# Turning the tail's exponentials with the fourth tile's, by sixteen moves inside SBUF, in an attention and feed-forward kernel

## The chip, the cores and the metric

The kernel runs on one core of one Trainium2 chip. The time is in device microseconds (us), the median of several executions. Next to it stands one profiled execution, with its own time and its span, which is the time from the first to the last instruction. Each query of the trace shows that execution.

The engines are named as in the profile: PE is TensorE (matrix products), PEld its weight loads, DVE is VectorE, ACT is ScalarE, POOL is GpSimd, and SP is SyncE, which here issues nearly all transfers (DMAs).

## The reference

```python
def _attn_ref(q, k, v, f):                    # q, k, v: 8 x 8 x 576 x 64; f: 8 x 8 x 576
    scores = scale * np.matmul(q, k.transpose(0, 1, 3, 2))
    cum = np.cumsum(np.log(np.clip(f, 0.0001, 1.0)), axis=-1)
    decay = cum[:, :, :, None] - cum[:, :, None, :]
    scores = np.where(causal, -1e9, scores + decay)
    attn = np.exp(scores - np.max(scores, axis=-1, keepdims=True))
    attn = attn / (np.sum(attn, axis=-1, keepdims=True) + 1e-09)
    return np.matmul(attn, v)

def _moe_ref(x, w_in, w_out, alpha):          # x: 4608 x 512; w_in: 512 x 2048; w_out: 2048 x 512
    h = x @ w_in
    g = np.maximum(h, 0.0) + alpha * np.minimum(h, 0.0)
    return g @ w_out
```

Eight batches of eight heads of causal attention with a decay feed a two-layer network. All values are float32.

## The kernel before

Attention is worked off in 32 pairs of heads (4 pairs in each of 8 batches), `attention(n)` for n from 0 to 31. The queries of a head are cut into four tiles of 128 and a tail of 64. The two tails of a pair are put together into one block of 128 rows, so that a pair has nine row blocks: four tiles for each head and one common tail. For a block the steps are these:

- TensorE makes the scores (for n of 4 and more from a split of Q and K into two parts each, three products).
- VectorE adds the decay (`Z` and `Zt`, spread to all rows by loads from DRAM) and finds the extreme of each row.
- ScalarE makes the exponentials and their row sums (`expo`, line 508).
- The exponentials are transposed, so that keys stand on the partitions, and go to the value product.

The transposing is done in two ways. The first is TensorE's: `blocks` (line 521) multiplies by the identity into a PSUM bank, and `evac` (lines 516 and 517) copies the bank to SBUF. Tiles 0, 1 and 2 and the tail (`tail`, lines 548 to 551) go this way. The second serves the fourth tile (i = 3) of a pair that is `turned`, which before the change are pairs 8 to 31: SP stores the exponentials of both heads to a DRAM buffer `ex` (line 659), loads them back in four loads (line 660) that put blocks of 32 rows side by side in `em`, and VectorE's stream transpose turns 32 x 32 blocks into `eT3_` (line 665). Keys then stand in another order on the partitions, and V is loaded a second time in that order (`vs`, line 497). In pairs 0 to 7 the fourth tile goes through TensorE too.

The value product of a pair (`prods_of`, line 687) is not run on its own: from pair 3 on it is put behind the scores of tile 2 of the next pair, in one step of TensorE (`stretch`, line 617).

When the four pairs of a batch are done, the first feed-forward product for that batch (`ffn1`, line 783) can run: 16 output blocks of 12 products of 512 columns. Its result goes through ScalarE and VectorE (lines 800 to 805) into a DRAM buffer (line 807). The second product (`ffn2`) comes after all attention. The weights `w_in` are converted at the start, by ScalarE, VectorE and GpSimd (`split64`, lines 306 to 329).

The order of the instructions on every engine is fixed when the kernel is built. `Plan.run` (line 115) places the steps one after the other: of the steps that are ready first it takes the one of the smallest key. It reckons a duration for each step, 400 ns or so for an issue on SP, and for transfers one common channel with a rate (line 160). A `Ring` hands out the buffers. On the chip the engines keep the order and wait for each other with semaphores.

Names that the text below uses: `eT` are transposed exponentials, `vr` is V, `rq` and `rk` are the loads of Q and K, `rd` and `ri` carry the reciprocals of the row sums, `hd` the results of the first product, `xx` and `wi` are the operands of the first feed-forward product, `turn` is the step with the stream transpose.

Of the kernel before, what the change touches and what calls it, by code (L numbers as in the profile page):

```python
# [29 lines left out]
NX = (8, B * NP)  # L30
# [53 lines left out]
class Plan:  # L84
# [30 lines left out]
    def run(self):  # L115
# [7 lines left out]
        while left:  # L123
# [63 lines left out]
def attention_moe(  # L187
    ctx: ExitStack,
    tc: tile.TileContext,
    qq: bass.AP,  # L190
    kk: bass.AP,
    vv: bass.AP,
    vs: bass.AP,
# [20 lines left out]
    ex = [dram.tile([2, 128, 512], F32, name=f"ex{i}") for i in range(2)]  # L214
# [32 lines left out]
    rrq = ring(sp, 2, [128, QW], F32, "rq")  # L247
    rrk = ring(sp, 2, [128, S], F32, "rk")
    rZ = Ring(Store([(sp.tile([128, 2, ZW], F32, name=f"Z{i}"), sp.tile([128, S], F32, name=f"Zt{i}")) for i in range(2)]))
    rvr = ring(sp, 2, [128, 5, 2, D], F32, "vr")  # L250
    rT1 = ring(sp, 3, [128, 384], F32, "eT1_")
    rT2 = ring(sp, 4, [128, 4, 192], F32, "eT2_")
# [5 lines left out]
    re3 = ring(sp, 1, [128, 2, 512], F32, "e3_")  # L258
# [5 lines left out]
    rwr = ring(sp, 2, [128, 512], U64, "wr")  # L264
    rwa = ring(sp, 1, [128, 512], U32, "wa")
# [7 lines left out]
    wbf = sp.tile([128, 512], BF16, name="wbf")  # L273
    sel = sp.tile([9, 6, 128], F32, name="sel")
# [150 lines left out]
    def load_n(n, held):  # L425
# [4 lines left out]
        bq, bk, bZ = Buf(rrq), Buf(rrk), Buf(rZ)  # L430
        kq = -99 if first else -59 if n == 1 else kl
        dq = [] if first else [o_scan]
        l_q = op("SP", 450, lambda: sy.dma_start(bq.t, qq[b, p]), kq, dq, [bq], kb=320)
        l_k = op("SP", 450, lambda: sy.dma_start(bk.t, kk[b, p]), kq, dq, [bk], kb=288)
        Z, Zt = (lambda: bZ.t[0]), (lambda: bZ.t[1])
        rz = []
        for h in range(2):
            if first:
# [12 lines left out]
        if first:  # L451
# [13 lines left out]
        if n < NN:  # L465
            held += [bq, bk]
            return [l_q, l_k], rz, rt, bZ, [(lambda: bq.t, lambda: bk.t)]
# [3 lines left out]
        for hi, lo, raw, ld, w in ((Qh, Ql, bq, l_q, QW), (Kh, Kl, bk, l_k, S)):  # L471
            o1 = op("ACT", c_acs(w), lambda hi=hi, raw=raw: ac.activation(hi(), raw.t, AF.Copy), kc, [ld], [raw, bQ])  # L472
            o2 = op("POOL", c_po(w), lambda hi=hi, lo=lo, raw=raw: po.tensor_tensor(lo(), raw.t, hi().bitcast(F32), ALU.subtract), kc, [o1], [raw, bQ])  # L473
            out += [o1, o2]
# [3 lines left out]
    waiting, behind, later_x = [], [], []  # L478

    def attention(n):  # L480
# [9 lines left out]
        bv = Buf(rvr)  # L490
        l_v = op("SP", 400, lambda: sy.dma_start(bv.t, vv[b, p]), kl + 1, [o_scan], [bv], kb=320)
        nt_ = 3 if n >= NN else 4
        bT1, bT2 = [Buf(rT1) for _ in range(2)], [Buf(rT2) for _ in range(2)]
        b3, bT3, turned = Buf(re3), Buf(rT3), NX[0] <= n < NX[1]
        if turned:
            bm, bvs = Buf(rm3), Buf(rvs)
            l_s = op("SP", 400, lambda: sy.dma_start(bvs.t, vs[b, p]), kl + 12, [o_scan], [bvs], kb=256)
# [27 lines left out]

        def tail(st):

            bt = Buf(re)
            prev = None
            for g in range(2):  # L530
# [9 lines left out]
                def red(bS=bS, ks=ks, g=g):  # L540
                    ve.tensor_tensor_reduce(out=bt.t[:, ks], in0=bS.t[:, :288], in1=bZ.t[1][:, ks],  # L541
                                            scale=-0.125, scalar=lo()[:, 9:10] if g else 3.0e38, op0=ALU.add, op1=ALU.min,
                                            accum_out=lo()[:, 4:5] if g else lo()[:, 9:10])
# [16 lines left out]
        def quick(bR, r_, key):  # L560
# [11 lines left out]
            q_ = op("PE", 1400, prods, key, [r_, o_sel], bB + [bR])  # L572
            for c0, c1 in ((0, 512), (512, S)):
# [30 lines left out]
        def stretch(tiles, st):  # L604
# [16 lines left out]
            s_0.append(s)  # L621
            done(s)
# [4 lines left out]
        def tile(h, i, st, bS, s, c0):  # L627
# [4 lines left out]
            at = (lambda t: t[:, h]) if i == 3 else (lambda t: t)  # L632
# [21 lines left out]
            if i == 3 and turned:  # L654
                if h == 0:
                    return
                d = ex[n % 2]
                key = k0 + 7.8
                o_ = op("SP", 400, lambda: sy.dma_start(d.rearrange("h q k -> q h k"), b3.t), key, [be[0][3][1], nm], [b3], kb=512)
                got = [op("SP", 400, lambda k=k: sy.dma_start(  # L660
                    bm.t[32 * k : 32 * k + 32], d[:, :, 128 * k : 128 * k + 128].rearrange("h (a c) s -> c (h a) s", c=32)),
                    key + 0.1, [o_], [bm], kb=128) for k in range(4)]
                for h_ in range(2):
                    def turn(h_=h_):
                        ve.transpose(bT3.t[:, h_].rearrange("p s (a c) -> p a s c", a=4),
                                     bm.t[:, 4 * h_ : 4 * h_ + 4].rearrange("p a (s r) -> p a s r", r=32))

                    e3.append(op("DVE", c_tr(512), turn, k0 + 13.5, got, [bm, bT3]))
                return
            if i >= 2:  # L670
# [3 lines left out]
                def tr2():  # L674
                    blocks(bT.t, 0, at(b1.t), range(i + 1))
                    if last:
                        pe.transpose(bT.t[0:64, 384:512], bt.t[:, 512:S], ident)  # L677

                t = op("PE", (i + 1 + last) * 109, tr2, st + 0.3, [nm, o_id] + ([nt] if last else []), [bT, b1] + ([bt] if last else []))
                to, tb = ((lambda: bT3.t[:, h]), bT3) if i == 3 else ((lambda: bT2[h].t[:, 0 : i + 1, 0:128]), bT2[h])  # L680
# [6 lines left out]
        def prods_of(r, out):  # L687

            def pv():
                both = []  # L690
                o = out()
                for h in range(2):
                    e1_, e2_ = bT1[h].t, bT2[h].t
                    if r == 0:
                        both.append([(0, 0, 256, e1_[:, 0:256]), (1, 128, 256, e1_[:, 256:384])])
                    else:
                        both.append([(j, 0, 128, e2_[:, j, 0:128]) for j in range(3)]
# [118 lines left out]
    for fc in range(NF):  # L816
        load_w_in(fc)
# [294 lines left out]
```

## Time and profile before

| | us |
|---|---|
| median of 3 runs | 1072.73 |
| lowest and highest run | 1070.98, 1072.88 |
| profiled execution, its time | 1073.41 |
| profiled execution, its span | 1071.6 |
| TensorE busy | 1054.9 |
| VectorE busy | 738.6 |
| ScalarE busy | 675.0 |
| GpSimd busy | 280.5 |

Busy time is the time in which an engine has at least one instruction running. Matrix products are pipelined: their recorded durations overlap, so the distance from the start of one to the start of the next is a better price than the duration. A row of the grouped view gives line, engine, operation, what is written and read, the shape and the count, and then the busy time, the mean duration, and the idle time just before with what ended it. The mean granted clock of TensorE is 0.992.

### The profile page before, as it was taken

What the parts mean: (1) busy time and instruction counts of PE and PEld (TensorE: products, weight loads), DVE (VectorE), ACT (ScalarE), POOL (GpSimd) and SP (SyncE); (2) the same over time, 40 slices, a digit from 0 to 9 for tenths busy, and PEclk for the clock granted to TensorE, in tenths of its full rate; (3) what the DMA queues carried; (4) which work ended last, traced back from release to release, by engine and by line L of the source; (5) the groups of instructions that cost most, each with busy time, mean ns of one, the idle gap of its engine ahead of it and who ended that gap; (6) DMA issues with size and microseconds to landing.
All of it is one profiled execution on the core that took longest, in us unless ns stands there. A gap on an engine that the chain in (4) does not pass through costs nothing.

```text
span 1071.6 us, 22543 instructions
## 1 busy us (share of the span) xinstructions
PE 1054.9 (98%) x8132; PEld 916.7 (86%) x8132; DVE 738.6 (69%) x1680; ACT 675.0 (63%) x1590; POOL 280.5 (26%) x407
## 2 busy tenths in 40 slices
PE   8889989999999999999999999999999999999998
PEld 5678867888888888888788888899999999999998
DVE  6788864555544545545544599779988898989994
ACT  6879877786766766667655375656454554646551
POOL 6578574553433434344221000000000000000000
PEclk9989999999999999999999999999999999999999
DMA  6967778987887986886763666464444443444411
GB/s 181 268 194 235 225 217 232 271 264 238 253 237 214 259 241 203 242 247 212 215 198 129 204 214 225 167 199 139 136 126 132 137 137 120 138 130 126 140 60 40
DMA packets 152441, 202.15 MB, mean 189 GB/s; under 512 B 18930, under 2 KB 89481, under 8 KB 152329
## 3 DMA queue, kind: packets, MB, share of 16 engines
q1 hardware_dynamic: 152041, 200.51, 61.3%
q8 instruction: 64, 1.05, 0.4%
q14 instruction: 48, 0.39, 0.1%
q10 hardware_dynamic: 288, 0.20, 0.1%
HBM read 139.55 MB, written 61.11 MB: 187 GB/s over the span
## 4 chain that ended last, share of the span: by engine, by line
PE 92%; DMA 2%; POOL 2%; DVE 1%; issue 1%; ACT 1%; SPq 0%; DVEq 0%; POOLq 0%
PE bank L332 86%; PE bank L521 5%; DMA Z<-c 2%; PE bank L392 1%; POOL Z L447 1%; DMA wr<-in_w_in_dram 0%; POOL wi L328 0%; POOL Z L448 0%; PE bank L677 0%; DVE eT L516 0%; DVE wa L322 0%; POOL Z L449 0%; ACT e L508 0%; POOL Ql L473 0%; POOL Kl L473 0%
## 5 line engine op out<-in xcount | busy, mean ns | idle before, releaser
L332 PE MATMUL bank<-xx,wi 128*128 128x512 f32 x1728 | 428.4, 397 | 2.3 <-ACT wi L327 1.8
L332 PEld LDWEIGHTS bank<-xx,wi 128*128 128x128 f32 x1728 | 314.4, 188 | 68.7 <-issue 4.8
L805 DVE SCALAR_TENSOR_TENSOR hs<-bank,sa,hs 128x512 f32<-128x512 f32 x96 | 71.2, 743 | 109.9 <-ACT hs L803 109.8
L332 PE MATMUL bank<-wot,xx 128*128 128x256 f32 x1008 | 123.9, 283 | 0.0
L332 PE MATMUL bank<-wi,xx 128*128 128x256 f32 x1008 | 123.9, 283 | 0.0
L332 PEld LDWEIGHTS bank<-wot,xx 128*128 128x128 f32 x1008 | 122.3, 192 | 0.0
L332 PEld LDWEIGHTS bank<-wi,xx 128*128 128x128 f32 x1008 | 122.3, 192 | 0.0
L508 ACT ACTIVATE e<-e,st 128x512 f32<-128x512 f32 (+2 forms) x160 | 109.2, 685 | 4.2 <-DVE st L541 2.0
L803 ACT ACTIVATE hs<-bank,ab 128x512 f32<-128x512 f32 x96 | 66.0, 688 | 63.4 <-PE bank L332 62.6
L517 ACT ACTIVATE eT<-bank 128x384 f32<-128x384 f32 (+2 forms) x192 | 83.3, 461 | 34.7 <-PE bank L332 20.1
L725 POOL TENSOR_TENSOR xx<-xs,xx 128x256 fp32r<-128x256 f32 x64 | 49.0, 783 | 136.6 <-ACT xx L723 136.4
L473 POOL TENSOR_TENSOR Ql<-rq,Qh 128x640 fp32r<-128x640 f32 x28 | 45.1, 1611 | 137.8 <-ACT Qh L472 89.7
L332 PE MATMUL bank<-eT,vr 128*64 128x128 f32 (+2 forms) x1408 | 80.0, 263 | 0.2 <-DVE eT L516 0.2
L332 PEld LDWEIGHTS bank<-eT,vr 128*64 128x64 f32 x1408 | 63.9, 138 | 14.1 <-issue 7.1
L447 POOL TENSOR_TENSOR Z<-Z,tri 128x384 f32<-128x384 f32 x64 | 60.0, 945 | 45.5 <-DMA Z<-c 31.2
L999 ACT ACTIVATE xx<-gx 128x1024 fp32r<-128x1024 f32 x48 | 50.8, 1058 | 30.8 <-PE bank L332 15.1
L521 PEld LDWEIGHTS bank<-ident,e 128*128 128x128 f32 x384 | 46.9, 146 | 20.5 <-issue 5.3
L521 PE MATMUL bank<-ident,e 128*128 128x128 f32 x384 | 62.2, 287 | 1.9 <-DVE st L639 1.6
L1002 DVE TENSOR_TENSOR xx<-gx,xx 128x1024 fp32r<-128x1024 f32 x48 | 58.6, 1220 | 7.4 <-ACT xx L999 7.4
L332 PE MATMUL bank<-wi,gh 128*128 128x256 f32 x504 | 62.4, 283 | 0.0
L332 PE MATMUL bank<-wot,gh 128*128 128x256 f32 x504 | 62.4, 283 | 0.0
L332 PEld LDWEIGHTS bank<-wot,gh 128*128 128x128 f32 x504 | 61.4, 192 | 0.1
(140 smaller groups left out, 1777.6 us busy)
## 6 DMA issues: line engine op xcount, KB each, us to landing
hd<-hs SPq DMA_DIRECT2D x144, 256.0 KB
wx<-hd SPq DMA_DIRECT2D x47, 512.0 KB
Z<-c SPq DMA_DIRECT2D x62, 256.0 KB
hr<-hd SPq DMA_DIRECT2D x25, 512.0 KB
ex<-e SPq DMA_DIRECT2D x24, 512.0 KB
em<-ex SPq DMA_DIRECT2D x96, 128.0 KB
rq<-in_qq_dram SPq DMA_DIRECT2D x32, 320.0 KB
vr<-in_vv_dram SPq DMA_DIRECT2D x32, 320.0 KB
```

Of the source, the lines that this page charges most:

```text
L332: pe.matmul(o, lhsT, rhs, start=start, stop=stop)
L392: op("PE", 800, lambda: [pe.matmul(bw.t, wbf[:, 0:128], wbf, start=True, stop=True) for _ in range(3)], -200, [o_wbf], [bw])
L447: m1 = op("POOL", c_po(128 * 3), lambda z4=z4: po.tensor_tensor(z4()[:, 6:9], z4()[:, 0:3], tb(3), ALU.add), kc + 0.1, got + [o_mask], [bZ])
L473: o2 = op("POOL", c_po(w), lambda hi=hi, lo=lo, raw=raw: po.tensor_tensor(lo(), raw.t, hi().bitcast(F32), ALU.subtract), kc, [o1], [raw, bQ])
L508: ex = op("ACT", c_exp(w), lambda: ac.activation(at(bt.t)[:, :w], at(bt.t)[:, :w], AF.Exp, bias=lo()[:, col : col + 1], scale=-1.0, accum_ ...
L517: return op("ACT", c_act(w), lambda: ac.activation(dst(), src(), AF.Copy), key, deps, [bank] + bufs)
L521: pe.transpose(t[:, c : c + 128], src[:, 128 * j : 128 * j + 128], ident)
L725: xl = op("POOL", c_po(256), lambda r=r, t0=t0: po.tensor_tensor(bx.t[:, 1, t0 : t0 + 256], bxs[r].t[:, 0:256], bx.t[:, 0, t0 : t0 + 256]. ...
L803: cp = op("ACT", c_act(512), lambda bh=bh, bs=bs, fc=fc: ac.activation(bs.t, bh.t, AF.Relu, scale=ab[:, fc : fc + 1]), -1000, [last, o_sg] ...
L805: cp = op("DVE", c_dve(512), lambda bh=bh, bs=bs, fc=fc: ve.scalar_tensor_tensor(bs.t, bh.t, sa[:, fc : fc + 1], bs.t, ALU.mult, ALU.add), ...
L999: his.append(op("ACT", c_acs(128 * GW * (j1 - j0)), lambda j0=j0, j1=j1, src=src, o_=o_: ac.activation(o_(0, j0, j1), src(), AF.Copy), key ...
L1002: rdy.append(op("DVE", c_dve(128 * GW * (j1 - j0)), lambda j0=j0, j1=j1, src=src, o_=o_: ve.tensor_tensor(o_(1, j0, j1), src(), o_(0, j0, ...
```

## The change

- Pairs 9 to 31 are `turned` in place of 8 to 31.
- In a turned pair the tail's exponentials are written beside the fourth tile's, in one buffer of 1024 + 576 columns. The first 512 columns of the tail are turned together with the fourth tile. The last 64 go through TensorE as before.
- The store to DRAM and the four loads become sixteen transfers from SBUF to SBUF, one for each source group of 32 partitions and each block of 128 columns. VectorE turns the tail's part with two more stream transposes.
- In the value product of a turned pair, the fourth tile's and the tail's columns stand side by side, so that one product of 192 columns takes the place of one of 128 and one of 64.
- Q and K come in one array and, from pair 4 on, in one load. A turned pair loads V in both orders (four blocks of each, one shared) in one load.
- The scratch of the weights' conversion gives room for `em` when the conversion is over (`wr`). When the value product of pair 8 is done, the buffers of `eT2_` become two buffers for a whole pair's tile 2 and a second buffer for the fourth tile (`swap`).
- The planner reckons with a rate of 220 in place of 280 in the first 90 us.
- The step `spread` is switched off.

```diff
-NX = (8, B * NP)
+FAR = 90.0
+NX = (9, B * NP)
+NQ = 4
...
-                self.chan = max(self.chan, s + 1.4) + o.kb / 280.0
+                self.chan = max(self.chan, s + 1.4) + o.kb / (220.0 if s < FAR else 280.0)
...
-    rT3 = ring(sp, 1, [128, 2, 4, 128], F32, "eT3_")
-    rm3 = ring(sp, 1, [128, 8, 128], F32, "em")
-    rvs = ring(sp, 1, [128, 4, 2, D], F32, "vs")
+    rT3 = ring(sp, 1, [128, 4, 384], F32, "eT3_")
+    wr = sp.tile([128, 1280], U64, name="wr")
+    wf = wr.bitcast(F32)
+    rm3 = Ring(Store([]))
+    em = wf[:, 0:1536].rearrange("p (k s) -> p k s", s=128)
...
-        l_q = op("SP", 450, lambda: sy.dma_start(bq.t, qq[b, p]), kq, dq, [bq], kb=320)
-        l_k = op("SP", 450, lambda: sy.dma_start(bk.t, kk[b, p]), kq, dq, [bk], kb=288)
+        l_qk = [op("SP", 450, lambda c0=c0, c1=c1: sy.dma_start(bqk.t[:, c0:c1], qk[b, p][:, c0:c1]), kq, dq, [bqk], kb=(c1 - c0) / 2)
+                for c0, c1 in (((0, QW), (QW, QW + S)) if n < NQ else ((0, QW + S),))]
...
+        if turned:
+            l_v = op("SP", 400, lambda: sy.dma_start(bv.t, vt[b, p]), kl + 12, [o_scan], [bv], kb=512)
+        else:
+            l_v = op("SP", 400, lambda: sy.dma_start(bv.t[:, 0:5], vv[b, p]), kl + 1, [o_scan], [bv], kb=320)
...
-            nt = expo(bt, S, 4, st + 0.6, [prev])
+            nt = expo(bt, S, 4, st + 0.6, [prev], tail_of)
+            if turned:
+                return bt, nt
             bTt = Buf(rT)
             tt = op("PE", 4 * 109, lambda: blocks(bTt.t, 0, bt.t, range(4)), st + 1.3, [nt, o_id], [bTt, bt])
...
-                o_ = op("SP", 400, lambda: sy.dma_start(d.rearrange("h q k -> q h k"), b3.t), key, [be[0][3][1], nm], [b3], kb=512)
-                got = [op("SP", 400, lambda k=k: sy.dma_start(
-                    bm.t[32 * k : 32 * k + 32], d[:, :, 128 * k : 128 * k + 128].rearrange("h (a c) s -> c (h a) s", c=32)),
-                    key + 0.1, [o_], [bm], kb=128) for k in range(4)]
+                src = lambda a, k: b3.t[32 * a : 32 * a + 32, 0:1536].rearrange("p (g s) -> p g s", g=3)[:, :, 128 * k : 128 * k + 128]
+                dst = lambda a, k: bm.t[32 * k : 32 * k + 32].rearrange("p (g a) s -> p g a s", a=4)[:, :, a]
+                got = [op("SP", 400, lambda a=a, k=k: sy.dma_start(dst(a, k), src(a, k)), key + (4 * a + k) / 100,
+                          [be[0][3][1], nm, nt], [b3, bm], kb=64) for a in range(4) for k in range(4)]
...
+                            both.append(head + [(j + 4, 128, 320, t3[:, j]) for j in range(3)] + [(3, 256, 320, bT4.t[:, 64 * h : 64 * h + 64])]
+                                        + [(7, 128, 320, t3[:, 3])])
...
+    op("-", 0, lambda: rm3.store.items.append(em) or rm3.store.free.append((plan.t, 0)), 0, [o for v in w_ready.values() for o in v])
+    for n in range(NX[0], B * NP):
+        attention(n)
+        if n == NX[0]:
+            def swap():
+                for st, t in [(rT2b.store, t2s[:, i, 0:768].rearrange("p (h j q) -> p h j q", h=2, q=128)) for i in range(2)] + [
+                        (re3.store, t2s[:, 2:4].rearrange("p a n -> p (a n)"))]:
...
-    "vs": vq,
+    "vt": np.concatenate([vp[:, :, :, (0, 1, 2, 4)], vq], axis=3),
```

More of the change, by code (lines that the diff above doesn't have):

```diff
@@ L476, in load_n @@
         return out, rz, rt, bZ, [(Qh, Kh), (Qh, Kl), (Ql, Kh)]
-    waiting, behind, later_x = [], [], []
+    waiting, behind, later_x, quick_ops, value_ops = [], [], [], [], []
     def attention(n):
@@ L524, in attention @@
         e2, e3 = [[], []], []
+        tail_of = (lambda t: t[:, 1024 : 1024 + S]) if turned else (lambda t: t)
         def tail(st):
-            bt = Buf(re)
+            bt = b3 if turned else Buf(re)
             prev = None
@@ L749, in values @@
             todo = [prods_of(r, lambda r=r: bP[r].t) for r in (1, 0)]
-            return (bP + [bv] + bT1 + bT2 + [bT3, bT4] + ([bvs] if turned else []), lambda: [f_() for f_ in todo], v_deps(),
+            return (bP + [bv] + bT1 + (bT2[:1] if turned else bT2) + [bT3, bT4], lambda: [f_() for f_ in todo], v_deps(),
                     lambda o: [done_v(r, bP[r])(o) for r in (1, 0)])
@@ L813, in attention_moe @@
     o_sg = op("DVE", 800, signs, 0.6, [o_al, s_0[-1]])
-    for n in range(1, B * NP):
+    for n in range(1, NX[0]):
         attention(n)
```

126 lines of the change are left out of this document (78 added, 48 removed).

## The prediction, made before the changed kernel was run

> **What bounds the kernel now.** I read the page first, then busy time by stage, then TensorE's instructions in order of time for one steady pair, then the DMA queue and VectorE beside them.
>
> ```profile
> span 1071.6 us, 22543 instructions
> PE 1054.9 (98%) x8132; PEld 916.7 (86%) x8132; DVE 738.6 (69%) x1680; ACT 675.0 (63%) x1590; POOL 280.5 (26%) x407
> PE 92%; DMA 2%; POOL 2%; DVE 1%; issue 1%; ACT 1%; SPq 0%; DVEq 0%; POOLq 0%
> ```
>
> TensorE is busy 98% of the span, and the chain that ended last runs over it for 92%. By stage (PE, weight loads, DVE, ACT, POOL, granted clock, DMA share, GB/s):
>
> ```profile
> 0.00:180.00 180.00, 167.22 (x1309) 126.98 (x1309) 129.31 (x341) 141.11 (x393) 118.00 (x179) 0.95 0.74 222
> 180.00:560.00 380.00, 380.00 (x3054) 307.48 (x3053) 191.25 (x575) 262.06 (x723) 154.34 (x218) 1.00 0.80 236
> ...
> 50.00:60.00 10.00, 9.43 (x50) 6.59 (x50) 8.12 (x28) 9.55 (x27) 8.60 (x13) 0.66 0.68 216
> 60.00:70.00 10.00, 6.64 (x35) 5.40 (x35) 8.64 (x19) 5.62 (x19) 7.68 (x11) 0.70 0.83 252
> ```
>
> There are two regimes. Before 180 us TensorE stands idle for 12.8 us (180 - 167.22) and loses clock around 50 to 70 us: several engines bound it together. From 180 to 560 us, where nearly all pairs that the change touches run, it is busy 380.00 of 380 at clock 1.00; DVE, ACT and POOL have half, a third and more than half of their time free. There an instruction taken off TensorE is time taken off the run, as long as nothing new makes TensorE wait. One steady pair on TensorE (start, us, instruction, count), and the feed-forward product alone, in a stretch of 90 us that holds nothing else:
>
> ```profile
> 429.90 0.81 PE L521 MATMUL bank<-ident,es 128*128 128x128 f32 x6
> 430.47 1.63 PE L332 MATMUL bank<-xx,wi 128*128 128x512 f32 x6
> 431.95 0.60 PE L521 MATMUL bank<-ident,e 128*128 128x128 f32 x4
> 432.30 3.00 PE L332 MATMUL bank<-xx,wi 128*128 128x512 f32 x12
> 435.23 0.44 PE L332 MATMUL bank<-Kh,Qh 64*128 64x384 f32 x2
> ...
> 435.95 0.88 PE L332 MATMUL bank<-eT,vr 128*64 128x128 f32 x12
> 436.65 1.04 PE L332 MATMUL bank<-eT,vs 128*64 128x128 f32 x16
> 437.53 1.40 PE L332 MATMUL bank<-eT,vr 128*64 128x64 f32 x28
> 438.86 1.66 PE L332 MATMUL bank<-xx,wi 128*128 128x512 f32 x6
> ```
>
> ```profile
> L332 PE MATMUL bank<-xx,wi 128*128 128x512 f32 x399 | 90.6, 389 | 0.0
> ```
>
> Durations overlap, so I price by start to start. The four transposes at 431.95 are the tail's (line 548): the step that the change takes from TensorE.
>
> **Part 1, the tail's transposes (off TensorE in pairs 9 to 31, 23 pairs).** Now 430.47 to 435.23 holds 18 feed-forward products and the four transposes: 4.76 us. A product alone takes 90.6/399 = 0.227 us, and twelve of them followed by other work take 435.23 - 432.30 = 2.93, which is 0.21 over 12 x 0.227. Eighteen in a row would take 18 x 0.227 + 0.21 = 4.30. The step is worth 0.46 us: 0.35 for the slot (431.95 to 432.30) and 0.11 for switching to and fro. Ends: 0.35 if the switch stays, 0.46; I take 0.46, since feed-forward work stands on both sides. 23 x 0.46 = **-10.6 us** (end: -8.1).
>
> **Part 2, pair 8.** It was turned by DMA and is not any more, so the eight transposes of its fourth tile (two groups of four) return to TensorE: 2 x 0.46 = **+0.9 us**. Its tail's transposes stay.
>
> **Part 3, the value products.** Per head, three products of 128, four of 128 and five of 64 columns become three of 128, four of 192 and one of 64; the columns streamed are the same, and 56 recorded instructions become 40. From 435.95 on, the rows give 0.70 for 12 (58 ns), 0.88 for 16 (55 ns) and 1.33 for 28, of which four of 256 and four of 128 columns take some 0.66 at that rate, leaving 0.67/20 = 33 ns for one of 64, against 27.5 for half of 55. Twenty become four and sixteen widen by 64 columns: the gain is 16 x 5.5 ns = 0.09 us a pair, 2 us in all; the other end is nothing, as the columns are the same. I take **-0.5 us**, nearer the equal columns.
>
> **Part 4, sixteen moves in place of one store and four loads.** This is where a loss can come from: SP issues in order. One period of its queue, from one store of the exponentials to the next (435.24), VectorE's two transposes in it, and the prices over all pairs:
>
> ```profile
> 418.24 0.39 SPq L659 DMA_DIRECT2D ex<-e  x1
> 420.62 0.33 SPq L491 DMA_DIRECT2D vr<-in_vv_dram  x1
> 421.00 0.42 SPq L497 DMA_DIRECT2D vs<-in_vs_dram  x1
> 421.52 0.86 SPq L443 DMA_DIRECT2D Z<-c  x2
> 422.42 1.09 SPq L463 DMA_DIRECT2D Zt<-c  x2
> 423.62 2.18 SPq L660 DMA_DIRECT2D em<-ex  x4
> 426.51 0.35 SPq L433 DMA_DIRECT2D rq<-in_qq_dram  x1
> 427.74 0.35 SPq L434 DMA_DIRECT2D rk<-in_kk_dram  x1
> 428.30 0.31 SPq L591 DMA_DIRECT2D rd<-R  x1
> 428.80 0.34 SPq L807 DMA_DIRECT2D hd<-hs  x1
> 432.90 0.46 SPq L598 DMA_DIRECT2D ri<-rd  x1
> 433.44 0.54 SPq L807 DMA_DIRECT2D hd<-hs  x1
> 434.03 1.11 SPq L598 DMA_DIRECT2D ri<-rd  x2
> 435.24 0.53 SPq L659 DMA_DIRECT2D ex<-e  x1
> ```
>
> ```profile
> 431.48 0.71 DVE L665 STREAM_TRANSPOSE eT<-em 128x512 f32<-128x512 f32 x1 [2.71 <-DMA em<-ex]
> 432.12 0.71 DVE L805 SCALAR_TENSOR_TENSOR hs<-bank,sa,hs 128x512 f32<-128x512 f32 x1
> 432.75 0.70 DVE L665 STREAM_TRANSPOSE eT<-em 128x512 f32<-128x512 f32 x1
> ```
>
> ```profile
> L660 SPq DMA_DIRECT2D em<-ex x96: 303/449/1250, 154.6 to 575.1; - x96
> L665 DVE STREAM_TRANSPOSE eT<-em x48: 664/700/714, 160.8 to 580.4; 128x512 f32<-128x512 f32 x48
> ```
>
> In this period of 17.0 us the issues take 8.7 us. The change removes the store (0.39), four loads (2.18), one V (0.42) and the K (0.35), and adds 16 x 0.449 = 7.2: about 12.6 of 17.0. The queue stays under its period, with a quarter left.
>
> The path to the value product: now the store is issued at 418.24, the second transpose ends at 433.45, and the product starts at 435.95, a margin of 2.5 us. After: sixteen issues from 418.24 and the other V, Z and Zt issues between (0.33 + 0.86 + 1.09) reach 427.7. The last piece's landing is not in this trace. Upper end: the last load now, issued at 425.3 (423.62 + 2.18 - 0.55), is what VectorE still waited for at 431.48, so 6.2 us; lower end, an estimate: that scaled to 48 KB from 128 KB, 2.3 us. The transposes then begin at 430.0 to 433.9; two of 0.70, two half ones together about 0.70, and the 0.71 in between make 2.8 us, so they end at 432.8 to 436.7. The middle, 434.8, is ahead of 435.95; the late end costs 0.75 us a pair. A doubled round trip through DRAM is replaced by a longer queue, and the two about balance. Ends 0 and 23 x 0.75 = +17; I take **+1.5 us** for some pairs with less margin.
>
> One more row matters here: loads wait for landings that they do not depend on (engine, line, waited for: us in total, times, longest).
>
> ```profile
> SPq L434 <- DMA Z<-c: 5.2, 9, 1.0
> ```
>
> The K load reads and writes nothing of Z; SP holds it back until an older transfer has landed. Nine more issues a pair will meet that more often; it is in the 1.5 and in the first rival.
>
> The Trainium skill ("DMA: Bandwidth & Descriptors", Rules for kernel authors) says to coalesce small transfers, since under 64 KB one pays mostly overhead; by that rule the sixteen of 48 KB are the wrong shape. The row sides with it only in part: four loads of 128 KB were issued in 2.18 us, with others in flight, so overheads overlap and the issue is the price.
>
> **Parts 5, covered.** VectorE gains about 0.7 us a pair, in a stage where it is busy 191 of 380. ScalarE loses two evictions a pair:
>
> ```profile
> L517 ACT ACTIVATE eT<-bank 128x256 f32<-128x256 f32 x56 | 18.5, 385 | 4.9 <-PE bank L521 4.9
> ```
>
> Two times 0.385 off ScalarE, worth nothing while TensorE is full. Q with K in one load: Q's part lands later by K's share, some 1.1 us at the stage's 236 GB/s (288 KB more), against a planned lead of nine units (kl to kc); without that cover TensorE would wait up to 1.1 us a pair. V in both orders: 64 KB less. The second buffer for the fourth tile removes the wait of the next pair's reduction on SP's reads, and PSUM banks are freed by the tail: nothing on the path.
>
> **Part 6, before 180 us.** The hand planner now reckons with 220 instead of 280 in the first 90 us, pairs 4 to 8 load Q with K, and pair 8 no longer moves 1 MB around 147 to 157 us, while a Z load just there is on the chain:
>
> ```profile
> 143.95 7.71 DMA Z<-c
> ```
>
> The order of the queues there will differ, and no row tells which way. Ends: -6.4 (the clock lost in 50 to 70 us, 10 x 0.34 + 10 x 0.30, recovered) and +5 (one more such half-clock spell and 2 us of idle). I take **0**.
>
> **Sum.** -10.6 + 0.9 - 0.5 + 1.5 + 0 = -8.7 us. The profiled execution took 1073.41 us (span 1071.6 and 1.8 around it), so 1064.7 on its scale; the median of the runs shown is 1072.73, 0.7 lower: **1064.0 us**.
>
> **Rivals.**
> - *The burst makes the value products late (slower).* Place: SP's queue between the last exponential and the value product. For it: 12.6 of 17.0 us issued in order, landings that hold back unrelated issues, a margin of 2.5 us. Against: one landing instead of two in series. At the late end, +17 instead of +1.5: 1079.5 us. It decides from 0.46 us of waiting a pair, which eats Part 1.
> - *The early stage comes out worse*: +5, so 1069 us; *or better*: -6, so 1058 us. For both: 12.8 us of idle and the low clock there; against: the work there is nearly unchanged.
> - *The change doesn't do what it says*: the transposes go, and TensorE waits instead for Z, Q and K behind a busier DMA (share 0.80): 1072.7 us. Against: 256 KB less a pair for the exponentials and 64 KB less V.
> - *The sixteen pieces are served one at a time*: at 1.0 us instead of 0.449 each the last lands 8.8 us later, 6.3 past the margin, 23 x 6.3 = 145 us: about 1210 us. The four loads in 2.18 us speak against it. The rule cited above, taken at its word, is this case.
>
> **How the numbers follow.** Forecast 0.57, late value products 0.12, early stage worse 0.12, better 0.10, no effect 0.08, one at a time 0.01. Faster or slower counts from 0.2% (2.1 us), about what a measurement of this kernel can tell from no change. Faster: 0.57 + 0.10 + most of 0.12 = 0.77; same: 0.08 and a little of the early case, 0.10; slower 0.13. The range runs from 1057.5 (part of the better early stage) to 1073.5 (the worse one and no effect); outside lie the late value products and a part of the best case. The forecast alone: 1061 to 1067.
>
> **What would show it.** Transposes by identity from e: 384 become 300 (9 pairs x 18 + 23 x 6); value product records 1792 become 1424 (9 x 56 + 23 x 40); 368 moves of 48 KB in place of 24 stores and 96 loads; 92 stream transposes, 46 of them half as long. TensorE busy all of 180 to 560 us again, with the attention's end some 9 us earlier; rows of TensorE waiting for the stream transposes (line of turn) would show the first rival, idle time or clock in 0 to 180 us the second. The prediction is wrong if the feed-forward groups that close up do not shorten to 0.227 us each, or if the queue's waits on landings grow past its free quarter.

## The result, and the profile after

| | us |
|---|---|
| predicted | 1064.0 (1057.5 to 1073.5) |
| before, median of four runs | 1072.63 |
| changed kernel, median of four runs | **1144.49** (1141.6 to 1147.43) |
| ratio to before, 95% interval | 1.0673 (1.064 to 1.0707) |
| changed kernel, profiled execution and its span | 1146.14, 1144.4 |

The change makes the kernel 72 us slower, far outside the range. The head of the profile after the change, with the busy time of the engines, the granted clock in 40 slices, and the chain of work that ended last:

```profile
span 1144.4 us, 21861 instructions
PE 1075.9 (94%) x7680; PEld 923.4 (81%) x7680; DVE 747.5 (65%) x1724; ACT 663.4 (58%) x1546; POOL 280.0 (24%) x407
PEclk9989999899999899999998999999999999999999
PE 69%; SPq 11%; DMA 7%; DVE 7%; issue 3%; ACT 1%; POOL 1%; DVEq 0%; POOLq 0%; ACTq 0%
```

Before, the chain ran over PE for 92% and over SP's queue (SPq) for 0%. Now SP's queue has 11% of it, and TensorE stands idle for 1144.4 - 1075.9 = 68.5 us, against 1071.6 - 1054.9 = 16.7. So 51.8 of the 72.8 us that the span grew by are new idle time. The other 21.0 us are in the busy time, although 452 matrix products fewer are recorded. By stage (columns as in the prediction):

```profile
0.00:180.00 180.00, 169.03 (x1350) 129.74 (x1352) 130.73 (x343) 142.00 (x392) 119.07 (x179) 0.95 0.71 213
180.00:560.00 380.00, 338.46 (x2204) 265.17 (x2200) 167.34 (x516) 212.90 (x576) 131.42 (x187) 0.95 0.64 186
560.00:750.00 190.00, 177.59 (x984) 142.74 (x985) 108.92 (x246) 103.94 (x227) 29.51 (x41) 0.96 0.57 177
750.00:1144.40 394.40, 390.77 (x3148) 385.78 (x3146) 340.50 (x622) 204.56 (x352) 0.00 (x0) 1.00 0.41 129
```

The early stage is as before (167.22 busy, clock 0.95). From 180 to 560 us, where TensorE was busy for 380.00 of 380 at clock 1.00, it is now busy for 338.46 at clock 0.95. Every other engine and the DMA share went down too, from 0.80 to 0.64: none of these has become the bound. The same in stretches of 50 us, the first, the worst and the sum of the ten from 200 to 700:

```profile
200.00:250.00 50.00, 44.61 (x299) 34.81 (x297) 22.44 (x68) 27.34 (x74) 15.26 (x22) 0.93 0.60 179
...
600.00:650.00 50.00, 41.62 (x289) 32.21 (x290) 23.69 (x71) 24.68 (x70) 13.07 (x21) 0.90 0.49 140
...
sum 500.00, PE 448.27 PEld 352.60 DVE 223.73 ACT 271.93 POOL 152.79; mean PE 44.83 PEld 35.26 DVE 22.37 ACT 27.19 POOL 15.28
```

Idle time is 500 - 448.27 = 51.7 us. The ten clocks fall short of 1.00 by 0.53 together, which over 50 us each is, as an estimate, 26.5 us of lost clock. These 78 us are the damage; the work that the change takes off TensorE hides a part of it in the total.

What TensorE waits for (engine, line, waited for: us in total, times, longest):

```profile
PE bank L341 <- DVE eT L703: 44.2, 18, 5.3
PE bank L341 <- POOL xx L768: 10.6, 4, 3.0
```

Line 703 is the new pair of stream transposes for the tail, the last step ahead of the value product. VectorE has time to spare, so it is worth seeing what VectorE waits for. One pair on SP's queue in the changed kernel, from its first move to its last (line 694; start, us, instruction, count). `wr` is the room in which `em` now lies, and `eT__112` is the second buffer for a pair's exponentials, in the room of the former `eT2_`:

```profile
446.19 2.58 SPq L694 DMA_DIRECT2D wr<-eT__112  x4
448.88 0.53 SPq L850 DMA_DIRECT2D hd<-hs  x1
449.45 3.80 SPq L694 DMA_DIRECT2D wr<-eT__112  x6
453.35 0.54 SPq L515 DMA_DIRECT2D vr<-in_vt_dram  x1
453.93 1.87 SPq L694 DMA_DIRECT2D wr<-eT__112  x3
455.90 1.02 SPq L464 DMA_DIRECT2D Z<-c  x2
456.97 1.13 SPq L486 DMA_DIRECT2D Zt<-c  x2
458.14 1.30 SPq L694 DMA_DIRECT2D wr<-eT__112  x2
459.54 0.53 SPq L850 DMA_DIRECT2D hd<-hs  x1
460.17 0.48 SPq L630 DMA_DIRECT2D ri<-rd  x1
460.70 0.58 SPq L772 DMA_DIRECT2D xt<-xs  x1
461.33 1.12 SPq L630 DMA_DIRECT2D ri<-rd  x2
462.49 0.63 SPq L694 DMA_DIRECT2D wr<-eT__112  x1
```

The same pair on VectorE, and then on TensorE (the bracket is the idle time before, and what ended it):

```profile
466.16 0.71 DVE L700 STREAM_TRANSPOSE eT<-wr 128x512 f32<-128x512 f32 x1 [9.03 <-DMA wr<-eT__112]
...
468.35 0.76 DVE L703 STREAM_TRANSPOSE eT<-wr 128x256 f32<-128x256 f32 x2
```

```profile
465.15 0.88 PE L341 MATMUL bank<-eT__112,vr 128*64 128x128 f32 x12
468.83 4.06 PE L341 MATMUL bank<-eT,vr 128*64 128x192 f32 x28 [2.81 <-DVE eT L703]
```

And all engines right after that stop (columns as by stage above; the clock is the last but two):

```profile
469.00:472.00 3.00, 3.00 (x22) 2.37 (x24) 1.94 (x5) 0.99 (x2) 1.41 (x2) 0.50 0.25 55
```

SP issues with hardly a gap from 446.19 to 463.12. VectorE has stood idle for 9.03 us when the moves are in place, and TensorE stops for 2.81 us in the middle of the value product. After the stop the granted clock is 0.50, and the 28 products take 4.06 us; in the pair at 354.10 us, which did not stop, they took 2.24. So the extra busy time sits in the value products: the rows of line 341 that read `vr` are busy for 168.7 us over the run, against 122.5 in the first kernel of the next section, where TensorE does not wait for them. In 17 us the queue has sixteen moves, which take 10.2 us, and eleven other issues in between (this is one of the longer bursts; the 23 pairs have 11.5 to 18.3 us, with 2 to 11 other issues). The last three moves stand behind two loads each of `Z` and `Zt`, and the very last also behind a store of `hd`, one of `xt` and three loads of `ri`.

### The profile page after: what moved, and what is told of

It is laid out like the page before. It is cut to its first block, busy times and chain, and to the rows that moved or that the text cites. A ratio compares the mean times of both kernels' runs of the same rounds, so it can differ in the third digit from the quotient of the medians.

```text
span 1144.4 us, 21861 instructions
## 1 busy us (share of the span) xinstructions
PE 1075.9 (94%) x7680; PEld 923.4 (81%) x7680; DVE 747.5 (65%) x1724; ACT 663.4 (58%) x1546; POOL 280.0 (24%) x407
## 4 chain that ended last, share of the span: by engine, by line
PE 69%; SPq 11%; DMA 7%; DVE 7%; issue 3%; ACT 1%; POOL 1%; DVEq 0%; POOLq 0%; ACTq 0%
PE bank L341 65%; SPq L694 6%; PE bank L548 3%; DVE eT L700 2%; DMA wr<-eT__112 2%; SPq L486 2%; DVE hs L848 1%; DMA wr<-e 1%; SPq L630 1%; DMA Z<-c 1%; DMA ri<-rd 1%; SPq L464 1%; DMA hd<-hs 1%; SPq L850 1%; DVE eT L703 1%
## 5 line engine op out<-in xcount | busy, mean ns | idle before, releaser
L341 PEld LDWEIGHTS bank<-xx,wi 128*128 128x128 f32 x1728 | 317.6, 190 | 78.3 <-POOL xx L768 12.3
L700 DVE STREAM_TRANSPOSE eT<-wr 128x512 f32<-128x512 f32 x46 | 30.9, 696 | 170.8 <-DMA hd<-hs 50.7
L341 PE MATMUL bank<-eT,vr 128*64 128x192 f32 (+3 forms) x896 | 95.2, 360 | 44.2 <-DVE eT L703 44.2
L341 PEld LDWEIGHTS bank<-eT,vr 128*64 128x64 f32 x896 | 73.3, 164 | 61.7 <-DVE eT L703 48.6
L752 ACT ACTIVATE xs<-bank 128x320 f32<-128x320 f32 x64 | 25.6, 409 | 115.7 <-PE bank L341 100.1
L535 ACT ACTIVATE e<-e,st 128x384 f32<-128x384 f32 (+2 forms) x127 | 84.9, 672 | 4.1 <-DVE st L570 2.0
L496 POOL TENSOR_TENSOR Ql<-rqk,Qh 128x640 fp32r<-128x640 f32 x28 | 44.6, 1593 | 83.1 <-issue 60.4
L341 PE MATMUL bank<-Kh,Qh 64*128 64x128 f32 (+1 forms) x280 | 62.2, 371 | 0.1
```

The costliest lines, as they stand in the source:

```text
L341: pe.matmul(o, lhsT, rhs, start=start, stop=stop)
L535: ex = op("ACT", c_exp(w), lambda: ac.activation(at(bt.t)[:, :w], at(bt.t)[:, :w], AF.Exp, bias=lo()[:, col : col + 1], scale=-1.0, accum_ ...
L700: ve.transpose(o, bm.t[:, 4 * g : 4 * g + 4].rearrange("p a (s r) -> p a s r", r=32))
```

## The experiments

The theory after the result had two parts. A move between two places in SBUF holds SP's queue for longer than the prediction priced it, and the order of all engines, written with 400 ns for it, is late by that much in each pair. The rivals: the moves themselves are slow to land; the tail in the fourth tile, the swap of buffers or the joint loads are at fault; any sixteen issues would do it.

**Only the moves undone.** The tail stays with the fourth tile, and all else of the change stays too; a store of three groups to DRAM and four loads replace the sixteen moves.

```diff
-                got = [op("SP", 400, lambda a=a, k=k: sy.dma_start(dst(a, k), src(a, k)), key + (4 * a + k) / 100,
-                          [be[0][3][1], nm, nt], [b3, bm], kb=64) for a in range(4) for k in range(4)]
+                o_ = op("SP", 400, lambda: sy.dma_start(d.rearrange("g q k -> q g k"), ...), key, [be[0][3][1], nm, nt], [b3], kb=768)
+                got = [op("SP", 400, lambda k=k: sy.dma_start(
+                    bm.t[32 * k : 32 * k + 32], d[:, :, 128 * k : 128 * k + 128].rearrange("g (a c) s -> c (g a) s", c=32)),
+                    key + 0.1, [o_], [bm], kb=192) for k in range(4)]
```

> The sixteen moves alone are undone: the three groups (two heads' fourth tile and the tail) are stored to DRAM in one transfer and come back in four loads; all else is the changed kernel. Theory 1 (SP's queue: sixteen issues of 0.60 us each, where the sum had 0.449 and the planner 0.40, make the value products late): the loss goes and the saved transposes show, 1061 to 1067 us, TensorE's wait for the tail's turn under 3 us. Theory 2 (the rest of the change is at fault: joint loads, shared scratch, buffers): stays over 1100 us.

Measured: 1058.24 us, 0.9867 of before (0.9848 to 0.9886), 13.7 us faster than before and 86 us faster than with the moves. The stage from 180 to 560 us of this kernel:

```profile
180.00:560.00 380.00, 380.00 (x2711) 303.35 (x2709) 209.97 (x640) 257.92 (x708) 159.97 (x224) 1.00 0.93 261
```

TensorE is full again at clock 1.00, with DMA at 0.93: the moves alone made the loss, and the detour over DRAM is the better way. This kernel beats both others, and lies under the 1061 to 1067 that were expected; the planner's rate, below, has a part in that.

**The moves alone, in the kernel before.** The tail stays on TensorE, and only the fourth tile's store and loads become sixteen moves of two groups each.

```diff
-                o_ = op("SP", 400, lambda: sy.dma_start(d.rearrange("h q k -> q h k"), b3.t), ...)
-                got = [op("SP", 400, lambda k=k: sy.dma_start(bm.t[32 * k : 32 * k + 32], ...), ..., kb=128) for k in range(4)]
+                src = lambda a, k: b3.t[32 * a : 32 * a + 32, :, 128 * k : 128 * k + 128]
+                dst = lambda a, k: bm.t[32 * k : 32 * k + 32].rearrange("p (h a) s -> p h a s", a=4)[:, :, a]
+                got = [op("SP", 400, lambda a=a, k=k: sy.dma_start(dst(a, k), src(a, k)), ...) for a in range(4) for k in range(4)]
```

> The kernel before, with the fourth tile's store and four loads replaced by sixteen moves inside SBUF of two groups each (64 runs of 512 bytes in place of 96); the tail stays on TensorE. If a move's price on SP comes from its kind (SBUF to SBUF, 32 partitions), it is about 0.6 us again and the kernel loses much of what the change lost: 1110 to 1150 us. If it follows the number of runs, it is near 0.4 us and the time is 1070 to 1095 us. Theory 2 (rest of the change) expects 1072 us.

Measured: 1166.32 us, 1.088 (1.0858 to 1.0902), above the range that was expected. The loss comes without the tail, the swap and the joint loads. The moves of this kernel (duration in ns: least, median, most; start of the first and last):

```profile
L659 SPq DMA_DIRECT2D em<-e x384: 585/595/1827, 146.5 to 677.1; - x192
```

Those of the changed kernel move half as many bytes again, and the last line says how long a move is on its way:

```profile
L694 SPq DMA_DIRECT2D wr<-e x192: 586/597/1372, 160.4 to 658.8; - x192
L694 SPq DMA_DIRECT2D wr<-eT__112 x176: 585/598/1687, 178.3 to 641.7; - x176
...
DMA to landing us min/median/max: 1.9/2.0/5.5
```

A move holds the queue for 0.595 us with 32 KB and for 0.597 with 48 KB, so the price goes by the move and not by its bytes. Where the trace tells the landing, it comes 1.9 to 5.5 us after the issue, 2.0 in the median. The last move of the pair shown was issued at 462.49, and VectorE began at 466.16: 3.7 us of the 20.0 since the first move. Slow landing, the first rival, can explain only that part.

**The planner told the price.** The changed kernel with 700 ns in place of 400 for a move, so that the order on all engines is made for it.

```diff
-                got = [op("SP", 400, lambda a=a, k=k: sy.dma_start(dst(a, k), src(a, k)), ...
+                got = [op("SP", 700, lambda a=a, k=k: sy.dma_start(dst(a, k), src(a, k)), ...
```

> The planner's price of each of the sixteen moves is 0.70 us in place of 0.40; the transfers themselves are the same. If only the order was wrong (theory 1a), TensorE's waits for the tail's turn (44 us) mostly go and the time is 1070 to 1090 us. If SP's queue itself is too full (theory 1b; it was issuing for 309 of 400 us), the waits move elsewhere and the time stays over 1120 us.

Measured: 1102.49 us, 1.0289 (1.0252 to 1.0325), between the ranges of the two theories. The stage from 180 to 560 us, and what TensorE waits for most:

```profile
180.00:560.00 380.00, 360.67 (x2442) 284.46 (x2439) 189.35 (x557) 229.43 (x616) 141.98 (x198) 0.96 0.70 201
```

```profile
PE bank L341 <- POOL xx L768: 13.5, 6, 4.4
PE bank L341 <- ACT xx L766: 9.0, 4, 2.3
```

The waits for line 703 are gone from the list. The price that the planner is told is thus worth 1144.5 - 1102.5 = 42 us, and another 44 us, down to 1058.2, stay. TensorE now runs out of feed-forward work: it waits 13.5 + 9.0 = 22.5 us for `xx`, the normalized results of attention. I read this as attention itself going more slowly; no row shows it alone. The landing is quick in this kernel: in all 23 pairs VectorE begins to turn 2.0 to 3.1 us after the last move's issue (starts of lines 694 and 700).

**Half the moves.** The kernel above with eight moves a pair. It leaves out half of the rows of these exponentials, so it serves for its time alone.

```diff
-                          ... for a in range(4) for k in range(4)]
+                          ... for a in range(2) for k in range(4)]
```

> The told version with only eight of the sixteen moves; the other half of the rows stays as it was in the buffer, which is zeroed once (that part of the exponentials is left out). 8 x 0.65 = 5.2 us a pair less on SP. Theory 1b: SP is no longer full and the time falls to 1056 to 1070 us. Theory 2 (something else in the moves' way, as their landing): over 1085 us.

Measured: 1064.69 us, 0.9929 (0.9905 to 0.9952). The stage from 180 to 560 us:

```profile
180.00:560.00 380.00, 375.19 (x2620) 298.09 (x2617) 205.61 (x624) 254.29 (x690) 158.81 (x222) 1.00 0.65 195
```

Eight moves fewer bring back 38 of the 44 us. The durations of all issues on SP, summed from 220 to 540 us (320 us, 337 to 465 issues), show how full the queue is:

| kernel | SP issuing, us of 320 | share | time, us |
|---|---|---|---|
| before | 162 | 51% | 1072.6 |
| only the moves undone | 158 | 49% | 1058.2 |
| idle copy and cut store, below (one run) | 205 | 64% | 1079.2 |
| sixteen loads from DRAM, below (one run) | 213 | 67% | 1128.4 |
| eight moves, price told | 216 | 68% | 1064.7 |
| eleven idle moves to shared places, below | 228 | 71% | 1164.5 |
| four of sixteen on ScalarE's queue, below | 228 | 71% | 1103.3 |
| changed kernel | 247 | 77% | 1144.5 |
| twelve idle moves, price not told | 254 | 79% | 1138.1 |
| moves alone, in the kernel before | 257 | 80% | 1166.3 |
| twelve idle moves, price told | 262 | 82% | 1129.6 |
| sixteen moves, price told | 267 | 83% | 1102.5 |

With eight moves, at 68%, little is lost, and from 77% on every kernel here is slow. But the four other kernels between 64% and 71%, which come below, lose 21 to 106 us against 1058.2. The idle copy, at 64%, loses 21, and TensorE is busy for 367.51 of the 380 us from 180 to 560. So the share alone does not say how slow a kernel is: what the queue waits for and the order of work count as well. With eight moves, half of the transfers are gone as well as half of the issues, so this run does not part the two.

**Idle moves.** Moves that nobody waits for, beside the detour over DRAM. The first kernel has eleven that share destinations, so that SP stands waiting for one landing after the other, which mixes two costs:

```diff
+                for m in range(11):
+                    op("SP", 400, lambda m=m: sy.dma_start(wf[32 * (m % 4) : 32 * (m % 4) + 32, 2048:2432]..., bv.t[32 * (m // 4) : 32 * (m // 4) + 32, 0:3]), ...)
```

> The DRAM version with eleven more moves a turned pair (same shape as the sixteen, from V to scratch that nobody reads, at 0.40 us in the planner): as many issues as the change has, but no work depends on them. Theory 1 (time of issuing on SP's in-order queue): 11 x 0.6 = 6.6 us a pair more on SP, so TensorE waits again and the time is over 1110 us. Rival (the moves' landing or the longer way to the value product is what cost): 1056 to 1072 us.

Measured: 1164.52 us, 1.0863 (1.0835 to 1.0891). SP waited 39.8 us for the landings of its own idle moves, so these 106 us (1164.5 - 1058.2) do not price the issues alone. The next two kernels have twelve moves, each to a place of its own, once with 700 ns told to the planner and once with 400:

```diff
+                for m in range(12):
+                    op("SP", 700, lambda m=m: sy.dma_start(wf[..., 1536 + 256 * (m // 4) : 1792 + 256 * (m // 4)]..., bv.t[..., 0:2]), ...)
```

> The DRAM version with twelve moves a turned pair that nobody waits for (two runs a row, from V to scratch, each to its own place, so that none waits for another), reckoned by the planner at 0.70 us. Theory 1b (SP's queue too full, so that attention goes at SP's pace): about as slow as the told sixteen, 1085 to 1110 us. Rival (the moves' own chain to the value product is too long): 1058 to 1068 us.

> The same twelve idle moves, reckoned at 0.40 us. If the order that the planner makes with the low price is what costs 42 us (1144 against 1102), this is slower than the told one by 20 to 50 us; if that cost came from the value product's own wait on the moves, both are equal within 10 us.

Measured: 1129.56 us told, 1.0534 (1.0503 to 1.0565), and 1138.06 us not told, 1.0627 (1.0586 to 1.0668). From the kernel told the price, the idle moves and the stage:

```profile
L700 SPq DMA_DIRECT2D wr<-vr x276: 507/589/2449, 159.7 to 653.1; - x138
```

```profile
180.00:560.00 380.00, 343.82 (x2239) 269.16 (x2236) 171.88 (x521) 212.47 (x580) 132.69 (x187) 0.95 0.83 238
```

Twelve moves whose data nobody reads cost 71 us (1129.6 - 1058.2), more than was expected, so no wait for the moved data is needed for such a loss. What is left is SP's time to issue them, or the transfers themselves beside the others. The DMA share is 0.83, below the 0.93 of the kernel without them, so the DMA engines are not fuller than there; no run took the issues off SP and kept all else. Telling the higher price brings only 8.5 us here. By what was written ahead, that is the case in which the 42 us above came from the value product's own wait for the moves, for which the low price left too little room, and not from the low price as such.

**What an issue costs by its two sides.** The detour with its store cut into four of 32 partitions, and one idle copy of V inside SBUF of 128 partitions.

```diff
-                o_ = op("SP", 400, lambda: sy.dma_start(d..., b3.t[:, 0:1536]...), ..., kb=768)
+                o_ = [op("SP", 400, lambda a=a: sy.dma_start(d[:, 32 * a : 32 * a + 32]..., b3.t[32 * a : 32 * a + 32, 0:1536]...), ..., kb=192) for a in range(4)]
+                op("SP", 400, lambda: sy.dma_start(wf[:, 2048:2560]..., bv.t[:, 0:4]), ..., kb=256)
```

> The DRAM version, its store cut into four stores of 32 partitions each, and one needless copy of V a pair, 128 partitions inside SBUF. It prices single issues: if 32 partitions as a source make an issue dear, the stores take about 0.6 us; if it is two sides in SBUF, the copy takes about 0.6 us and the stores 0.37 us. The time itself is not the question (1058 to 1090 us).

One run: 1079.22 us. The stores of 32 partitions from one of its two buffers, and then its copy inside SBUF:

```profile
L694 SPq DMA_DIRECT2D ex<-e x48: 303/473/1832, 160.3 to 584.7; - x48
```

```profile
L697 SPq DMA_DIRECT2D wr<-vr x23: 494/644/1497, 165.5 to 586.1; - x23
```

And sixteen loads of 48 KB from DRAM, with the same destinations as the moves, after one store:

```diff
+                dst = lambda a, k: bm.t[32 * k : 32 * k + 32].rearrange("p (g a) s -> p g a s", a=4)[:, :, a]
-                got = [op("SP", 400, lambda k=k: ... for k in range(4)]
+                got = [op("SP", 400, lambda a=a, k=k: sy.dma_start(dst(a, k), d[:, 32 * a : 32 * a + 32, 128 * k : 128 * k + 128]...), ...) for a in range(4) for k in range(4)]
```

> The three groups are stored to DRAM once and come back in sixteen loads with the same destination pattern as the moves. If an issue is dear because both sides are SBUF, it falls to 0.45 us here and the time is near 1100 us; if it is dear by the pattern of the 32 partitions and three groups, it stays at 0.60 us and the time is 1150 us or more, as a round trip is added.

```profile
L697 SPq DMA_DIRECT2D wr<-ex x368: 302/428/1782, 167.5 to 649.9; - x184
```

One run: 1128.39 us. An issue with DRAM on one side takes 0.30 us at least and 0.43 to 0.47 in the median; one with both sides in SBUF takes 0.49 to 0.59 at least and 0.59 to 0.64 in the median. So it is the two sides in SBUF that go with the dear issue, and not the 32 partitions. Sixteen loads are cheaper to issue, and yet this kernel is slow. Its SP issues for only 213 of 320 us (67%), but besides it stands waiting for the store's landing, and behind it all else in the queue (SP's waits, then TensorE's):

```profile
SPq L697 <- DMA ex<-e: 29.6, 12, 4.9
```

```profile
PE bank L342 <- ACT xx L769: 29.8, 4, 8.5
PE bank L342 <- DVE eT L706: 12.7, 7, 3.9
```

How much of its 70 us comes from that wait, from the longer chain, and from an order made for other prices stays open.

**Four of the sixteen on ScalarE's queue**, price told:

```diff
-                          ... for a in range(4) for k in range(4)]
+                          ... for a in range(3) for k in range(4)]
+                sent = [op("ACT", 650, lambda k=k: ac.dma_start(dst(3, k), src(3, k)), ...) for k in range(4)]
```

> The sixteen moves with the planner told 0.70 us, four of them issued by ScalarE's queue. If SP's full queue holds the remaining 44 us (1102 against 1058), taking 2.4 us a pair off it gives 1070 to 1088 us. If landing or contention of the moves inside SBUF holds them, it stays at 1095 to 1110 us; if ScalarE cannot take 2.4 us a pair, over 1110 us.

Measured: 1103.32 us, 1.0295 (1.0264 to 1.0326), no better than the 1102.49 without it. By what was written ahead, this is the range for landing or contention of the moves inside SBUF. But ScalarE now has four moves of each pair in its own queue, and waits with them for the stream transposes of line 706 (its waits):

```profile
ACT hs L849 <- DVE eT L706: 23.4, 3, 9.8
```

The kernel without this edit has no such wait among ScalarE's nine largest. SP's issuing fell from 267 to 228 of 320 us without a gain, and whether ScalarE's wait ate it can't be told from this run. So it settles nothing on relief for SP, and contention of the moves with other transfers stays a rival for the last 44 us.

**The planner's rate, and a dearer SP.** Two edits to the kernel with the detour:

```diff
-FAR = 90.0
+FAR = 0.0
```

> The DRAM version with the planner's old rate of 280 in the first 90 us as well. If the new rate has a part in the gain (1058.2 against the summed 1062 to 1063), the time is 1060 to 1066 us; if not, 1056 to 1060 us.

```diff
-SLACK = {"DVE": 1.12, "ACT": 1.08, "POOL": 1.05}
+SLACK = {"DVE": 1.12, "ACT": 1.08, "POOL": 1.05, "SP": 1.15}
```

> The DRAM version with every issue on SP reckoned 15% dearer in the planner (0.46 for 0.40), as the trace has it. If the planner's order still suffers from the low price, 1050 to 1056 us; if TensorE is full anyway after 180 us, as the windows say, 1056 to 1062 us.

Measured: with the old rate 1064.01 us, 0.9927 (0.9903 to 0.9951), so the new rate is worth 5.8 us; with all SP issues reckoned 15% dearer 1059.8 us, 0.9888 (0.9862 to 0.9915), which can't be told from 1058.24.

## Why the prediction was wrong, step by step

**Part 4 failed, and alone decided.** It put the sixteen moves at +1.5 us; they cost 1144.5 - 1058.2 = 86. Four things in it were wrong:

- *The price.* I took 0.449 us from loads of `em` from DRAM as the nearest row. A move inside SBUF took 0.597. In the pair shown, the sixteen took 10.2 us in place of 7.2, which makes 3.0 us, more than the margin of 2.5 that I had counted. (The margin itself was read to 435.95, the first row of the value product; the first product that reads the turned tile stood at 436.65, so it was 3.2.)
- *What stands in between.* I counted five other issues, 2.3 us (V, Z and Zt). The pair shown had eleven issues, 16.9 - 10.2 = 6.7 us with the short gaps, since a queue that has fallen behind has `hd`, `ri` and `xt` due in it as well. Together the burst took 16.9 us, not 9.5. The landing was not the problem: at most 3.7 us in this pair, between the 2.3 and the 6.2 that I had allowed.
- *The share of the queue.* By the right price the period of 17.0 us would have held 8.7 - 3.3 + 16 x 0.597 = 14.9 us of issues (3.3 is what the change removes), 88% and not the 12.6 that I called "under its period, with a quarter left". The quarter left was no reserve: with eight moves, at 68%, the kernel lost 6 us against the one with the detour, and every kernel at 77% and more lost over 40.
- *The consequences of a wait.* The upper end, 0.75 us a pair, had only the wait itself. Some 26.5 us of lost clock follow it, and the order of all engines was made for 400 ns: telling the planner 700 brings 42 us.

Of the 86 us, the runs thus show that the moves make them and that 42 go when the planner is told. That the other 44 are SP's time is the best reading, with contention among the transfers not ruled out.

On the clock, the Trainium skill ("TensorE: Matmul & The Clock Gate", HAM oscillation — how this bites in real kernels) says that idle gaps of over some 3.4 us make the clock fall to half, over and over where a loop waits for its transfers each time. This case agrees in kind: the stretches with waits of up to 5.3 us show 0.90 to 0.97, and the same stretches before the change 1.00. On the length it differs. From 180 to 750 us the changed kernel's trace has 16 stops of TensorE of 2 us and more; after 13 of them, or late in them, the clock is 0.50 for 3.4 or 6.8 us. Nine of these 13 stops were shorter than 3.4 us, the shortest 2.09, while three of 2.21, 2.51 and 2.58 us left the clock at 1.00. So in this kernel a stop of 2 to 3 us may or may not cost clock, and 3.4 us is no safe bound.

**The rivals.** The late value product was the right rival, with a chance of 0.12 and with the right sign to look for (line of turn, 44.2 us), but its 1079.5 us were far too little. "One at a time" at 1.0 us a move, with a chance of 0.01, had the nearest mechanism, pieces that follow one another, at too high a price; what came one at a time was the issue, at 0.597 us, and its 1210 us are off on the other side. The bound that the first one gave, 0.46 us of waiting a pair, was passed: the trace has 44.2/23 = 1.9. I had weighed the second against the four loads issued in 2.18 us, which have their source in DRAM, and that kind of issue is the cheaper one. The Trainium skill ("DMA: Bandwidth & Descriptors", Rules for kernel authors) says to put many small transfers together, because under 64 KB one pays mostly overhead. The runs side with it: four loads of 192 KB behind one store of 768 KB (1058.24 us) beat sixteen pieces of 48 KB by 86 us. The overhead that the rows show is SP's time to issue; whether the transfers add to it was not parted.

**Parts 1 to 3 held.** Without the burst they can be seen, in the kernel with the moves undone. TensorE in one pair, at the value product and where the tail's transposes stood before:

```profile
408.38 0.88 PE L342 MATMUL bank<-eT__114,vr 128*64 128x128 f32 x12
409.09 2.24 PE L342 MATMUL bank<-eT,vr 128*64 128x192 f32 x28
411.25 1.66 PE L342 MATMUL bank<-xx,wi 128*128 128x512 f32 x6
...
420.90 7.08 PE L342 MATMUL bank<-xx,wi 128*128 128x512 f32 x30
427.91 0.44 PE L342 MATMUL bank<-Kh,Qh 64*128 64x384 f32 x2
```

Thirty feed-forward products in a row take 427.91 - 420.90 = 7.01 us, and 30 x 0.227 + 0.21 is 7.02: the closed-up group costs what Part 1 said, 0.227 us for each product. The value product takes 411.25 - 408.38 = 2.87 us against 2.91 before, 0.04 a pair and about 1 us in all, between Part 3's -0.5 and its end of -2. The count of transposes by identity from `e` is the 300 that was named. With the planner's old rate, so without Part 6, the kernel with the detour is 7.7 us faster than before (interval 5 to 10), where Parts 1 to 3 said 10.2; the detour of three groups is in that too.

**Part 6** was put at 0 between -6.4 and +5. In the kernel with the detour the new rate gave -5.8, near its good end, but not by the way that was named: from 50 to 70 us the clock is 0.66 and 0.77 there, against 0.66 and 0.70 before, so hardly any of that loss came back. What the traces show instead is TensorE's idle time from 90 to 180 us, 2.8 us with the old rate and none with the new, and another 1.2 us from 180 to 560; the rest is not placed. That the size came near the end is luck. **Part 5** was put at nothing and was covered: with the detour TensorE is busy for 380.00 of 380. (Its 1.1 us for K's share should be 1.2, from its own 288 KB and 236 GB/s.)

## What to carry to other kernels

Price an issue by a row with the same kind of both sides, and put it down as time of the queue that issues it, not of the transfer: a shorter way for the data can be a longer way for the queue. When one queue issues nearly all transfers, count all that it must issue in one period, at that price, and what each issue will wait for; here a quarter left over was no reserve, and the share alone did not order the times. And where a planner fixes the order, its price for a new step is part of the change: telling it 700 ns in place of 400, for what takes 597 sixteen times a pair, brought 42 of the 86 us here.

## What the hardware showed that I had not expected

- An issue on SP's queue with both sides in SBUF held the queue for 0.595 us in the median with 32 KB and 0.597 with 48 KB, never under 0.585. With the source in DRAM, the same destinations and 48 KB it was 0.302 at least and 0.428 in the median.
- The transfer of such a move was quick where the trace tells its landing: 2.0 us from issue to landing in the median (1.9 to 5.5), against 6.0 us (3.7 to 6.9) for the loads of 192 KB from DRAM in the kernel with the detour.
- Twelve moves a pair whose data nobody reads cost 71 us on a kernel whose SP had been issuing for half of the time.
- Stops of TensorE of 2.09 to 3.1 us were in nine cases enough for the clock to fall to 0.50 for at least 3.4 us, in the changed kernel.
